# A single-token attention kernel that streams 825 MB: last scores before the last value sums, longer wo rows, and a 14 : 18 split of the scores between VectorE and TensorE

## The chip, the cores and the metric

One core of a Trainium2 chip. The metric is the device time of one launch in microseconds (us), as the median of several launches. PE is the TensorE matmul engine, PEld its weight load, DVE VectorE, ACT ScalarE, SP the engine whose queue issues the DMAs. Runs are compared with runs of the kernel before on the same chip in the same rounds.

## The reference, cut to what matters

```
x: (1, 1, 640)   k_cache, v_cache: (1, 32 heads, 32768 keys, 192)   bf16
q   = layernorm(x) @ wq                              # 32 heads x 192
p   = softmax(q . k_cache * 192**-0.5)               # one query row per head
o   = p @ v_cache                                    # (32 * 192)
h   = x + o @ wo
out = h + relu(layernorm(h) @ w1) @ w2               # 640 -> 1536 -> 640
```

Each byte of the two caches is used once. They are 805 MB of the 825 MB that are read.

## The kernel before: the parts that matter

A load brings 8192 keys of one head: 128 partitions x 64 keys ("columns") x 192 values, 24,576 B per partition. It is worked on as two chunks of 32 columns. Of a chunk, DVE scores 12 columns (multiply by the broadcast query, then reduce), and PE scores 20 (transpose K, ACT copies the transposes from PSUM, then matmuls with q). The value sums `pv` of a chunk run on PE one chunk later. The last head ends in smaller loads of 40, 16 and 8 columns.

```
full = [(JL, [(J, 20), (J, 20)])] * (Sk // (P * JL))       # (columns, of them on PE)
ends = full[:-1] + [(40, [(20, 12), (20, 12)]), (16, [(16, 10)]), (8, [(8, 4)])]
NEND = 3
...
wo_view = A_wo.rearrange("(b p) n -> p b n", p=P)          # 3 rows of 1280 B per partition
...
# o_turn: the scaled outputs of two heads become three columns
for b in range(3):
    for i in range(2):
        nc.tensor.matmul(ps[:, b:b + 1], lhsT=src[:, i, b * P:(b + 1) * P], rhs=ident_f[0:2, i:i + 1], ...)
...
# main loop over chunks g
if end == 0 and c0 == 0:                  # the last three K, then the last three V, then w1 and w2
    for i in range(NEND): load_k(ld + i)
    for i in range(NEND): load_v(ld + i)
    load_w("w1", ...); load_w("w2", ...)
...
transposes(g)
if g > 0:
    pv(g - 1)
scores_pe(g)
sc = scores_dve(g)
...
exp_dve(g, sc)
# after the loop
den_mm(H - 1); den_rec(H - 1)
pv(G - 1)
o_scale(H - 1); o_turn(H - 1); project(H // 2 - 1)
# then the dense layers
```

The softmax here doesn't subtract the row's maximum and nothing guards it: scores larger than these inputs give would overflow.

Of the kernel before, what the change touches and what calls it, by code (L numbers as in the profile page):

```python
# [13 lines left out]
def kernel(  # L14
# [12 lines left out]
    nc = tc.nc  # L27
    P = nc.NUM_PARTITIONS

    Bsz, Sq, D = A_x.shape  # L30
    _, H, Sk, Dh = A_k_cache.shape
# [9 lines left out]
    JL = 64  # L41
    J = 32
# [2 lines left out]



    full = [(JL, [(J, 20), (J, 20)])] * (Sk // (P * JL))
    ends = full[:-1] + [(40, [(20, 12), (20, 12)]), (16, [(16, 10)]), (8, [(8, 4)])]
    NEND = 3  # L50
    loads = []
    chunks = []
    for h in range(H):
        k0 = c = 0
# [8 lines left out]
            k0 += P * jl  # L63
        assert k0 == Sk
    G = len(chunks)
    NCH = [sum(1 for q in chunks if q[0] == h) for h in range(H)]
    NCM = max(NCH)
    NBM = max(q[5] for q in chunks) * Dh // P
# [4 lines left out]
    vpool = ctx.enter_context(tc.tile_pool(name="vpool", bufs=3))  # L73
# [3 lines left out]
    tsb = ctx.enter_context(tc.tile_pool(name="tsb", bufs=2))  # L77
    prp = ctx.enter_context(tc.tile_pool(name="prp", bufs=1))
    scp = ctx.enter_context(tc.tile_pool(name="scp", bufs=3))
    pcp = ctx.enter_context(tc.tile_pool(name="pcp", bufs=3))  # L80
    small = ctx.enter_context(tc.tile_pool(name="small", bufs=2))
    tps = ctx.enter_context(tc.tile_pool(name="tps", bufs=3, space=bass.MemoryType.PSUM))
    sps = ctx.enter_context(tc.tile_pool(name="sps", bufs=1, space=bass.MemoryType.PSUM))
# [4 lines left out]
    def mm_bank(shape, dtype, name):  # L88
        return mps.tile(shape, dtype, tag="mm", name=name)

    k_hd = A_k_cache.rearrange("b h s d -> (b h) s d")
    v_hd = A_v_cache.rearrange("b h s d -> (b h) s d")
    wq_view = A_wq.rearrange("(c p) n -> p c n", p=P)
    wo_view = A_wo.rearrange("(b p) n -> p b n", p=P)


    x_row = const.tile([DT, P], bf16)
# [5 lines left out]
    vt_t = {}  # L103

    def load_wq(gq):
        t = wqp.tile([P, DT * QG * Dh], bf16, tag="wq", name="wq")
        t = t[:].rearrange("p (c n) -> p c n", c=DT)
        nc.sync.dma_start(out=t, in_=wq_view[:, :, gq * QG * Dh:(gq + 1) * QG * Dh])
        wq_t[gq] = t

    def load_wo(pr):
        t = wop.tile([P, 3, D], bf16, name="wo")
        nc.sync.dma_start(out=t[:], in_=wo_view[:, 3 * pr:3 * pr + 3, :])
        wo_t[pr] = t

    def load_part(ld, src, pool, tag, name):
        h, k0, jl = loads[ld]
        if ld == len(loads) - 1:
            pool, tag, size = wqp, "wq", DT * QG * Dh
        else:  # L120
            size = JL * Dh
        t = pool.tile([P, size], bf16, tag=tag, name=name)
        nc.sync.dma_start(out=t[:, 0:jl * Dh], in_=src[h, k0:k0 + P * jl, :].rearrange("(p j) d -> p (j d)", p=P))
        return t

    def load_k(ld):
        kt_t[ld] = load_part(ld, k_hd, kpool, "kt", "kt")

    def load_v(ld):
        vt_t[ld] = load_part(ld, v_hd, vpool, "vt", "vt")  # L130

    w_t = {}

    def load_w(name, src, pool, tag, pieces):
        n, N = src.shape[0] // P, src.shape[1]
        assert n * N <= JL * Dh and n % pieces == 0
        t = pool.tile([P, JL * Dh], bf16, tag=tag, name=tag)
        v = t[:, 0:n * N].rearrange("p (c n) -> p c n", n=N)
        for i in range(pieces):
            c0, c1 = i * n // pieces, (i + 1) * n // pieces  # L140
            nc.sync.dma_start(out=v[:, c0:c1], in_=src.rearrange("(c p) n -> p c n", p=P)[:, c0:c1])
        for c in range(n):
            w_t[name, c] = v[:, c, :]
# [6 lines left out]
    ident_f = const.tile([P, P], f32)  # L150
# [40 lines left out]
    with tc.manual_schedule():  # L191
# [19 lines left out]
        def q_spread(h):  # L211
            r = rows_e[h % 2]
            qbps = mm_bank([P, Dh + 4], f32, "qbps")
            nc.tensor.matmul(qbps[:, 0:Dh], lhsT=ones_row[:], rhs=r[0:1, 0:Dh], start=True, stop=True)
            for i in range(4):
                nc.tensor.matmul(qbps[:, Dh + i:Dh + i + 1], lhsT=r[0:1, i * P:(i + 1) * P],
                                 rhs=ones_row[0:1, 0:1], start=True, stop=True)
            qb = qbp.tile([P, Dh], bf16, name="qb")
            nc.scalar.copy(out=qb[:], in_=qbps[:, 0:Dh])
            qm = qbp.tile([P, 4], bf16, name="qm")  # L220
            nc.scalar.copy(out=qm[:], in_=qbps[:, Dh:Dh + 4])
            qb_t[h], qm_t[h] = qb, qm
# [6 lines left out]
        def transposes(g):  # L229
            h, c, ld, c0, jc, jp = chunks[g]  # L230
            kt = kt_t[ld]
            NB = jp * Dh // P
            kT = tsb.tile([P, NBM, P], bf16, name="kT")
            for b0 in range(0, NB, 8):
                nb = min(8, NB - b0)
                tp = tps.tile([P, 8, P], bf16, name="tp")
                for b in range(nb):
                    off = (c0 + jc - jp) * Dh + (b0 + b) * P
                    nc.tensor.transpose(out=tp[:, b, :], in_=kt[:, off:off + P], identity=ident_b[:])  # L239
                nc.scalar.copy(out=kT[:, b0:b0 + nb, :], in_=tp[:, 0:nb, :])  # L240
            kT_t[g] = kT
# [18 lines left out]
        def scores_dve(g):  # L260
            h, c, ld, c0, jc, jp = chunks[g]
            kt = kt_t[ld]
            JD = jc - jp
            qb = qb_t[h]
            pr = prp.tile([P, JDM, Dh], f32, name="pr")
            nc.vector.tensor_tensor(out=pr[:, 0:JD, :], in0=kt[:, c0 * Dh:(c0 + JD) * Dh].rearrange("p (j d) -> p j d", d=Dh),  # L266
                                    in1=qb[:].unsqueeze(1).to_broadcast([P, JD, Dh]), op=A.mult)
            sc = scp.tile([P, J], f32, name="sc")
            nc.vector.reduce_sum(out=sc[:, 0:JD], in_=pr[:, 0:JD, :], axis=mybir.AxisListType.X)  # L269
            return sc  # L270
# [9 lines left out]
        def pv(g):  # L280

            h, c, ld, c0, jc, jp = chunks[g]
            JD = jc - jp
            vt, pA, pB = vt_t[ld], pA_t.pop(g), pB_t.pop(g)
            if c == 0:
                o_t[h] = ops.tile([2, 2 * Dh], f32, name="o_ps")
            o = o_t[h]
            order = list(range(JD, jc, 2)) + list(range(0, JD, 2))
            for i, j in enumerate(order):
                p = pA[:, j:j + 2] if j < JD else pB[:, j - JD:j - JD + 2]  # L290
                first = c == 0 and i == 0
                last = c == NCH[h] - 1 and i == len(order) - 1
                nc.tensor.matmul(o[:], lhsT=p, rhs=vt[:, (c0 + j) * Dh:(c0 + j + 2) * Dh], start=first, stop=last)  # L293
# [25 lines left out]
        def o_turn(h):  # L319
            if h % 2 == 0:  # L320
                return
            pr = h // 2
            src = o_pair[pr % 2]
            ps = mm_bank([P, 3], f32, "oT_ps")
            for b in range(3):
                for i in range(2):
                    nc.tensor.matmul(ps[:, b:b + 1], lhsT=src[:, i, b * P:(b + 1) * P], rhs=ident_f[0:2, i:i + 1],  # L327
                                     start=(i == 0), stop=(i == 1))
            oT = small.tile([P, 3], bf16, tag="oT", name="oT")
            nc.vector.tensor_copy(out=oT[:], in_=ps[:])  # L330
            oT_t[pr] = oT
# [12 lines left out]
        q_spread(0)  # L344
        for g in range(G):
            h, c, ld, c0, jc, jp = chunks[g]
            end = ld - (len(loads) - NEND)
            if end == 0 and c0 == 0:
                for i in range(NEND):
                    load_k(ld + i)  # L350
                for i in range(NEND):
                    load_v(ld + i)

                load_w("w1", B_w1, kpool, "kt", 1)
                load_w("w2", B_w2, vpool, "vt", 2)
            elif end < 0 and c0 == 0 and g > 0:
                load_k(ld)
                load_v(ld)
            if c == 1 and h % 2 == 0:
                load_wo(h // 2)  # L360
            if c == 3 and h % QG == QG - 2 and h + 2 < H:
                load_wq(h // QG + 1)
            transposes(g)
            if g > 0:
                pv(g - 1)
            scores_pe(g)
            sc = scores_dve(g)
            if c == 0 and h > 0:
                den_mm(h - 1)
                den_rec(h - 1)  # L370
                o_scale(h - 1)
            if c == 1 and h > 0:
                o_turn(h - 1)
            if c == 2 and h > 0 and h % 2 == 0:
                project(h // 2 - 1)
            if c == 4 and h + 1 < H:
                q_rows(h + 1)
            if c == 5 and h + 1 < H:
                q_spread(h + 1)
            exp_dve(g, sc)  # L380
        den_mm(H - 1)
        den_rec(H - 1)
        pv(G - 1)
        o_scale(H - 1)
        o_turn(H - 1)
        project(H // 2 - 1)
# [55 lines left out]
```

## Time and profile before

| | kernel before |
|---|---|
| time, median of 3 | 1954.45 us (1954.04 to 1954.61) |
| profiled span | 1952.3 us |
| moved by DMA | 827.85 MB, mean 424 GB/s |
| PE, DVE, ACT busy | 82%, 69%, 55% |
| last full K load landed ("L4") | 1912.08 |
| last value sum done | 1940.65 (28.57 after L4) |
| from there to the end | 11.65 us |

The busy shares are averages over a run in which every engine waits for loads. What sets the end are the three last rows: when the stream of loads delivers the last full K load, how long the work on the last five loads takes after it, and a closing chain of small dependent steps.

### The profile page before, as it was taken

What the parts mean: (1) busy time and instruction counts of PE and PEld (TensorE: products, weight loads), DVE (VectorE), ACT (ScalarE), POOL (GpSimd) and SP (SyncE); (2) the same over time, 40 slices, a digit from 0 to 9 for tenths busy, and PEclk for the clock granted to TensorE, in tenths of its full rate; (3) what the DMA queues carried; (4) which work ended last, traced back from release to release, by engine and by line L of the source; (5) the groups of instructions that cost most, each with busy time, mean ns of one, the idle gap of its engine ahead of it and who ended that gap; (6) DMA issues with size and microseconds to landing.
All of it is one profiled execution on the core that took longest, in us unless ns stands there. A gap on an engine that the chain in (4) does not pass through costs nothing.

```text
span 1952.3 us, 44906 instructions
## 1 busy us (share of the span) xinstructions
PE 1594.4 (82%) x20392; PEld 1122.4 (57%) x20392; DVE 1338.0 (69%) x654; ACT 1067.5 (55%) x2223; POOL 0.7 (0%) x6
## 2 busy tenths in 40 slices
PE   6887887878788788787888877888788887887887
PEld 4655565555556556555555655655555565565655
DVE  5766777667666676676767666777666766676675
ACT  4555555555555555555655555555555555555554
POOL 0000000000000000000000000000000000000000
PEclk9989889989998889998988989899899989898998
DMA  9999999999999999999999999999999999999996
GB/s 405 431 429 429 430 431 430 429 429 431 431 430 428 430 431 430 431 429 431 430 429 430 429 431 430 430 431 424 431 431 428 425 421 431 427 430 426 430 421 253
DMA packets 51522, 827.85 MB, mean 424 GB/s; under 512 B 4612, under 2 KB 17412, under 8 KB 18564
## 3 DMA queue, kind: packets, MB, share of 16 engines
q1 hardware_dynamic: 51332, 824.99, 99.0%
q8 instruction: 159, 2.61, 0.5%
q14 instruction: 31, 0.25, 0.0%
HBM read 824.97 MB, written 0.00 MB: 423 GB/s over the span
## 4 chain that ended last, share of the span: by engine, by line
DMA 77%; PE 17%; ACT 4%; DVE 1%; issue 1%; SPq 0%; ACTq 0%
DMA kt<-in_A_k_cache_dram 75%; PE o_ps L293 8%; PE tp L239 6%; ACT kT L240 3%; DMA vt<-in_A_v_cache_dram 1%; DVE pr L266 1%; PE sp L249 1%; PE sp L253 1%; PE sp L251 1%; PE qps L205 0%; ACT pA L276 0%; ACT pB L256 0%; DVE o_pair L314 0%; PE oT_ps L327 0%; ACT row_e L208 0%
## 5 line engine op out<-in xcount | busy, mean ns | idle before, releaser
L240 ACT COPY kT<-tp 128x1024 bf16<-128x1024 bf16 (+1 forms) x1025 | 905.2, 966 | 343.1 <-PE tp L239 340.2
L266 DVE TENSOR_TENSOR pr<-kt,qb 128x2304 f32<-128x2304 bf16 (+1 forms) x258 | 655.0, 2539 | 483.3 <-DMA kt<-in_A_k_cache_dram 479.9
L239 PE MATMUL tp<-ident_b,kt 128*128 128x128 bf16 x7677 | 599.3, 242 | 342.8 <-DMA kt<-in_A_k_cache_dram 269.7
L239 PEld LDWEIGHTS <-kt 128*128 128x128 bf16 x7677 | 531.1, 110 | 381.2 <-DMA kt<-in_A_k_cache_dram 280.2
L269 DVE TENSOR_REDUCE sc<-pr 128x12 f32<-128x2304 f32 (+1 forms) x258 | 654.3, 2536 | 27.6 <-ACT kT L240 1.4
L293 PE MATMUL o_ps<-vt,pB 128*2 128x384 bf16 x2559 | 498.8, 346 | 2.6 <-DMA vt<-in_A_v_cache_dram 2.6
L293 PEld LDWEIGHTS <-pB 128*2 128x2 bf16 x2559 | 203.8, 87 | 226.9 <-issue 65.9
L256 ACT ACTIVATE pB<-sp 128x20 bf16<-128x20 f32 (+1 forms) x258 | 48.4, 188 | 492.4 <-PE sp L253 492.4
L293 PE MATMUL o_ps<-vt,pA 128*2 128x384 bf16 x1537 | 291.9, 326 | 0.0
L249 PEld LDWEIGHTS <-kT 128*128 128x128 bf16 x2559 | 196.1, 96 | 85.7 <-issue 84.7
L249 PE MATMUL sp<-qm,kT 128*128 128x2 bf16 x2559 | 218.6, 164 | 0.5 <-ACT kT L240 0.5
L251 PE MATMUL sp<-qm,kT 128*128 128x1 bf16 x2559 | 215.0, 163 | 0.0
L253 PE MATMUL sp<-qm,kT 128*128 128x1 bf16 x2559 | 215.0, 163 | 0.0
L251 PEld LDWEIGHTS <-kT 128*128 128x128 bf16 x2559 | 198.7, 96 | 0.0
L293 PEld LDWEIGHTS <-pA 128*2 128x2 bf16 x1537 | 129.1, 84 | 120.8
L253 PEld LDWEIGHTS <-kT 128*128 128x128 bf16 x2559 | 197.4, 96 | 0.0
L276 ACT ACTIVATE pA<-sc 128x12 bf16<-128x12 f32 (+1 forms) x258 | 52.8, 205 | 0.0
L256 ACT ACTIVATION_READ_ACCUMULATOR pB<-sp 128x1 f32 x258 | 50.1, 194 | 0.0
L276 ACT ACTIVATION_READ_ACCUMULATOR pA<-sc 128x1 f32 x258 | 49.3, 191 | 0.0
L305 DVE TENSOR_REDUCE rec<-den 128x1 f32<-128x20 f32 x32 | 5.7, 179 | 60.2 <-PE den L299 60.2
L315 ACT ACTIVATE o_pair<-o_ps,rec 2x192 f32<-2x192 f32 x32 | 13.2, 412 | 26.9 <-DVE o_pair L314 26.9
L327 PE MATMUL oT_ps<-ident_f,o_pair 2*128 2x1 f32 x192 | 24.2, 247 | 0.1
(60 smaller groups left out, 191.4 us busy)
## 6 DMA issues: line engine op xcount, KB each, us to landing
kt<-in_A_k_cache_dram SPq DMA_DIRECT2D x127, 3072.0 KB, 35.7
vt<-in_A_v_cache_dram SPq DMA_DIRECT2D x127, 3072.0 KB, 31.4
wq<-in_A_wq_dram SPq DMA_DIRECT2D x8, 960.0 KB, 34.7
wo<-in_A_wo_dram SPq DMA_DIRECT2D x16, 480.0 KB, 31.2
kt<-in_A_k_cache_dram SPq DMA_DIRECT2D x1, 1920.0 KB, 30.7
vt<-in_A_v_cache_dram SPq DMA_DIRECT2D x1, 1920.0 KB, 25.4
kt<-in_B_w_dram SPq DMA_DIRECT2D x1, 1920.0 KB, 17.1
vt<-in_B_w_dram SPq DMA_DIRECT2D x2, 960.0 KB, 13.3
```

The source lines that it names most:

```text
L239: nc.tensor.transpose(out=tp[:, b, :], in_=kt[:, off:off + P], identity=ident_b[:])
L240: nc.scalar.copy(out=kT[:, b0:b0 + nb, :], in_=tp[:, 0:nb, :])
L249: nc.tensor.matmul(sp[:, 2 * i:2 * i + 2], lhsT=kT[:, 3 * i + 1, :], rhs=qm[:, 1:3], start=True, stop=False, skip_group_check=True)
L251: nc.tensor.matmul(sp[:, 2 * i:2 * i + 1], lhsT=kT[:, 3 * i, :], rhs=qm[:, 0:1], start=False, stop=False, skip_group_check=True)
L253: nc.tensor.matmul(sp[:, 2 * i + 1:2 * i + 2], lhsT=kT[:, 3 * i + 2, :], rhs=qm[:, 3:4], start=False, stop=True, skip_group_check=True)
L256: nc.scalar.activation(out=pB[:, 0:JP], in_=sp[:, 0:JP], func=F.Exp, scale=SCALE, accum_out=dsums[:, h, 2 * c + 1:2 * c + 2])
L266: nc.vector.tensor_tensor(out=pr[:, 0:JD, :], in0=kt[:, c0 * Dh:(c0 + JD) * Dh].rearrange("p (j d) -> p j d", d=Dh), in1=qb[:].unsqueeze(1 ...
L269: nc.vector.reduce_sum(out=sc[:, 0:JD], in_=pr[:, 0:JD, :], axis=mybir.AxisListType.X)
L276: nc.scalar.activation(out=pA[:, 0:JD], in_=sc[:, 0:JD], func=F.Exp, scale=SCALE, accum_out=dsums[:, h, 2 * c:2 * c + 1])
L293: nc.tensor.matmul(o[:], lhsT=p, rhs=vt[:, (c0 + j) * Dh:(c0 + j + 2) * Dh], start=first, stop=last)
L315: nc.scalar.activation(out=dst[:, 1, n0:n0 + Dh], in_=o[:, Dh:2 * Dh], func=F.Copy, scale=s[0:2, 1:2])
L327: nc.tensor.matmul(ps[:, b:b + 1], lhsT=src[:, i, b * P:(b + 1) * P], rhs=ident_f[0:2, i:i + 1], start=(i == 0), stop=(i == 1))
```

## The change

Its intent: take PE work off (14 of 32 columns on DVE), move wo in fewer, longer packets, and let no K work of the last loads wait for V. The V load of the last 40 columns (the first of the last three V loads) is also split in two.

```diff
-    full = [(JL, [(J, 20), (J, 20)])] * (Sk // (P * JL))
+    full = [(JL, [(J, 18), (J, 18)])] * (Sk // (P * JL))
...
+    ENDS = [g for g in range(G) if chunks[g][2] >= len(loads) - NEND]
...
-    wo_view = A_wo.rearrange("(b p) n -> p b n", p=P)
+    wo_view = A_wo.rearrange("(g p b) n -> g p b n", p=P, b=3)
...
     def load_v(ld):
-        vt_t[ld] = load_part(ld, v_hd, vpool, "vt", "vt")
+        parts = [(q[3], q[3] + q[4]) for q in chunks if q[2] == ld] if ld >= len(loads) - NEND else None
+        vt_t[ld] = load_part(ld, v_hd, vpool, "vt", "vt", parts)      # one DMA per chunk
...
-  lhsT=src[:, i, b * P:(b + 1) * P]
+  lhsT=src[:, i, b:3 * P:3]
...
-            if g > 0:
+            if g > 0 and g - 1 not in ENDS:
                 pv(g - 1)
...
-        pv(G - 1)
+        for g in ENDS:
+            pv(g)
```

(The pool of probabilities grows from 3 to 6 buffers, for the deferred sums.)

More of the change, by code (lines that the diff above doesn't have):

```diff
@@ L79 @@
     scp = ctx.enter_context(tc.tile_pool(name="scp", bufs=3))
-    pcp = ctx.enter_context(tc.tile_pool(name="pcp", bufs=3))
+    pcp = ctx.enter_context(tc.tile_pool(name="pcp", bufs=6))
     small = ctx.enter_context(tc.tile_pool(name="small", bufs=2))
@@ L112, in load_wo, with load_part @@
         t = wop.tile([P, 3, D], bf16, name="wo")
-        nc.sync.dma_start(out=t[:], in_=wo_view[:, 3 * pr:3 * pr + 3, :])
+        nc.sync.dma_start(out=t[:], in_=wo_view[pr])
         wo_t[pr] = t
-    def load_part(ld, src, pool, tag, name):
+    def load_part(ld, src, pool, tag, name, parts=None):
         h, k0, jl = loads[ld]
@@ L122, in load_part @@
         t = pool.tile([P, size], bf16, tag=tag, name=name)
-        nc.sync.dma_start(out=t[:, 0:jl * Dh], in_=src[h, k0:k0 + P * jl, :].rearrange("(p j) d -> p (j d)", p=P))
+        rows = src[h, k0:k0 + P * jl, :].rearrange("(p j) d -> p (j d)", p=P)
+        for j0, j1 in parts or [(0, jl)]:
+            nc.sync.dma_start(out=t[:, j0 * Dh:j1 * Dh], in_=rows[:, j0 * Dh:j1 * Dh])
         return t
@@ L326, in o_turn @@
                 for i in range(2):
-                    nc.tensor.matmul(ps[:, b:b + 1], lhsT=src[:, i, b * P:(b + 1) * P], rhs=ident_f[0:2, i:i + 1],
+                    nc.tensor.matmul(ps[:, b:b + 1], lhsT=src[:, i, b:3 * P:3], rhs=ident_f[0:2, i:i + 1],
                                      start=(i == 0), stop=(i == 1))
```

## The prediction

> **What bounds the kernel now.** First the 40 slices of the span, then the DMA queues, then the chain that ended last.
>
> ```profile
> PE   6887887878788788787888877888788887887887
> DVE  5766777667666676676767666777666766676675
> DMA  9999999999999999999999999999999999999996
> GB/s 405 431 429 429 430 431 430 429 429 431 431 430 428 430 431 430 431 429 431 430 429 430 429 431 430 430 431 424 431 431 428 425 421 431 427 430 426 430 421 253
> ...
> q1 hardware_dynamic: 51332, 824.99, 99.0%
> q8 instruction: 159, 2.61, 0.5%
> ...
> DMA 77%; PE 17%; ACT 4%; DVE 1%; issue 1%; SPq 0%; ACTq 0%
> ```
>
> The DMA row is full and some 430 GB/s move in every slice but the first and the last: 825 MB at 430 GB/s are 1918 of the 1952.3 us. PE and DVE stand at 6 to 8 tenths. So two things only can move the time: what the DMA engines have to do, and the last slice, where they run dry.
>
> The last slice I read from the timeline and from windows. Columns of the windows: stretch, length, busy (instructions) of PE, its weight loads, DVE, ACT, POOL, then granted clock, DMA share, GB/s.
>
> ```profile
> 1893.43 12.61 SPq L123 DMA_DIRECT2D kt<-in_A_k_cache_dram  x3
> 1906.10 13.78 SPq L123 DMA_DIRECT2D vt<-in_A_v_cache_dram  x3
> ...
> 1912.17 2.56 DVE L266 TENSOR_TENSOR pr<-kt,qb 128x2304 f32<-128x2304 bf16 x1 [4.36 <-DMA kt<-in_A_k_cache_dram]
> 1914.83 2.55 DVE L269 TENSOR_REDUCE sc<-pr 128x12 f32<-128x2304 f32 x1
> ...
> 1924.21 1.76 DVE L266 TENSOR_TENSOR pr<-kt,qb 128x1536 f32<-128x1536 bf16 x1 [1.57 <-DMA kt<-in_A_k_cache_dram]
> ...
> 1910.40:1913.80 3.40, 1.68 (x16) 1.68 (x17) 1.63 (x1) 0.55 (x1) 0.00 (x0) 0.50 0.98 419
> 1913.80:1917.20 3.40, 3.40 (x22) 2.15 (x21) 3.30 (x2) 3.00 (x4) 0.00 (x0) 0.50 0.58 248
> 1917.20:1924.00 6.80, 6.54 (x84) 4.32 (x83) 5.30 (x3) 4.02 (x8) 0.00 (x0) 1.00 0.75 272
> 1924.00:1931.00 7.00, 6.80 (x105) 4.72 (x103) 6.55 (x4) 3.80 (x12) 0.00 (x0) 1.00 0.95 366
> ...
> PE o_ps L293 <- DMA vt<-in_A_v_cache_dram: 0.8, 1, 0.8
> ```
>
> The reader is to see: the last full K load lands just before 1912.17 (call this moment L4). From there PE is busy almost without a break (6.54 of 6.80, 6.80 of 7.00 us), and the wait for V that the change wants to avoid is 0.8 us, once. PE's value sums end at 1940.65, and a fixed chain of 11.65 us (turn, projection, layer norm, two dense layers, output) leads to 1952.3.
>
> **A second bound, hidden in the 99%.** The trace records the sixteen completion updates of each load, one per DMA engine. For the first K load they lie at 13.0 to 13.6 us. For the K load issued at 1874.79 eight lie at 1890.3 to 1894.6 and eight at 1910.3 to 1912.1. Half the engines have fallen some 20 us behind. They are those that also fetch instructions: the late ones step back in turn, by about 1.4 us at a time. 159 fetches over 8 engines are 20 each, 28 us. A load counts as landed with its slowest engine, so these eight set the pace. In the packet records they are back to back to the end: from 1912 the remaining loads land at 1919.4, 1924.1, 1926.1, 1927.0, 1931.5, 1933.4, 1934.4, 1939.1, 1941.5 and 1944.0, as their sizes ask.
>
> **What the Trainium skill says.** "Runtime: NRT & Kernel Launch", Instruction fetch mechanics: an engine's instructions come in 16 KiB blocks of 256, over a DMA queue of its own, and the cost is mostly hidden. The count agrees (PE's 40,315 program rows / 256 = 157.5; the page shows 159 packets); hidden it is not here, at 1.4 us on a saturated engine. "DMA: Bandwidth & Descriptors", Why small descriptors are slow: a fixed cost per packet. The trace agrees and shows it small: from start to start a 1280-B packet takes 52 ns, a 3072-B one 118 ns, a 24,576-B one 908 ns. "TensorE: Matmul & The Clock Gate", Part 1: half clock after an idle window of about 3.4 us, full clock after a busy one. The trace agrees, but is stricter: at 1910.4 the clock fell to 0.50 after a window in which PE was still half busy, and came back at 1917.2. "VectorE: DVE Perf Modes", The perf-mode tier table: a reduce runs at one element per cycle. Here 2304 elements take 2.55 us and 1536 take 1.75, thus 0.2 us per column of 192.
>
> **Part by part.**
> 1. wo rows of 3840 B. 16 loads x 24 packets x 52 ns = 20.0 us per engine become 16 x 8 x about 146 ns (3 x 1280 B at the rate of large packets, 142 ns, and some 4 ns) = 18.7. All of it lies on the bound: -1.3 us.
> 2. 18 instead of 20 columns on PE. Each of some 254 full chunks loses 3 transposes and 3 score matmuls, each with its weight load: 12 rows, 3,048 in all, matching the program's 37,267 PE rows. 3,048 / 256 = 12 fetches fewer, 1.5 on each of the eight slow engines, at 1.4 us: -2.1 to -2.3 us, on the bound. PE's own saving (about 0.25 us a chunk) only lengthens its waits.
> 3. 14 instead of 12 columns on DVE. Two instructions of 2.95 instead of 2.55 us: a load costs DVE 4 x 2.95 + 0.3 = 12.1 us, where a K and V pair arrives every 14.6 us. DVE goes from 69% to about 80%, still beside the loads. K buffers come free 1.2 us later, at 9.1 after landing, against a backlog of more than 20 us on the slow engines: nothing.
> 4. Last scores first. L4 comes 3.5 us earlier, near 1908.6, from parts 1 and 2. Then, in us after L4. DVE: two full chunks to 12.2 (the next K piece lands at 12.0), two of 8 columns to 19.5, then 22.4 and 24.4. PE: first full chunk at half clock, as now, to 7.6; second to 13.1; first short chunk with the last undeferred value sums to 17.6. After that nothing fills PE while ACT copies transposes: short chunk two ends at 21.0, the next at 24.0, the last at 25.7; the exponentials at 26.2. Only then come the denominators (0.4 us) and 32 deferred value sums at 0.173 us: 5.5 us, where today 4 sums (0.75 us) follow. V is there (22.3). End at 32, against 28.6 today (1940.65 - 1912.08): +3.4 us.
> 5. Clock. Between 18.7 and 26 PE would be busy 30 to 48% of a window, less than the half that cost it the clock at 1910.4. Then the deferred sums start at half clock, and regain it after 3.5 to 5 us, as the trace shows for other restarts: about +2.2 us more, and +0.4 in the last scores.
>
> Sum: -3.5 + 3.4 + 2.6 = +2.5 us if the clock falls; about -0.1 if it does not; about -1.5 if it does not and the first chunk runs at full clock too (end at 30.7 to 31.1, set by DVE).
>
> **The rivals.** (a) The intent holds: V waits held up K work and the end shrinks by 3 to 6 us. For it: the chain of waits runs through the V load that landed at 1931.5, with 9.1 us of work behind it. Against: the wait itself is 0.8 us and PE's work is not reduced, only moved behind the last score. It would make 1949 to 1951. (b) The loads set the end: w2 lands at 1944.0 and its use starts at 1947.5, so it has 3.5 us to spare; with the loads 3.5 us earlier this stays hidden, and nothing changes. (c) DVE becomes the bound in the steady part: 12.1 of 14.6 us speaks against it; a head's first chunk adds under 1 us. If it did, 1% or more would be lost. (d) The stream gains nothing: another engine of the eight keeps its fetches, or packets cost as before; then the end's +2.5 to +6 stands alone, 1957 to 1960.
>
> **Range and chances.** Three to one for the falling clock: 0.75 x 2.5 + 0.25 x -0.8 = +1.7. I take off 0.7 for the chance of (a), since the change was made with it in mind: +1.0, thus 1955.5 us. The range 1951.5 to 1959.0 holds (a) in its milder form and most of (d). Two per cent are 39 us, more than the whole end after L4's 28.6 us, so beyond 2% either way only a bound I have not seen could do it.
>
> **What would show it.** Step 1 and 2: the page shows near 146 instruction packets; the loads before the end land 3 to 4 us earlier, at the same GB/s of 430. Step 3: DVE near 80%, groups of 2688 elements at 2.95 us, no wait of PE for it before the end. Step 4: the last scores are through some 26 us after L4, then one unbroken run of 32 value sums. Step 5: granted clock of 0.5 in that run, sums of over 0.3 us. I am wrong if the clock stays full there, if the sums wait for V, or if the loads are not earlier.

## The result, and the profile after

The changed kernel took 1955.64 us (median of 4, 1955.30 to 1956.15), the kernel before on the same chip 1954.24 (1953.99 to 1954.61): 1.4 us more. The ratio is 1.0007, with a 95% interval of 0.999 to 1.0025: the same at the 2% threshold.

The page of the changed kernel, slices, queues and chain:

```profile
DVE  6877888778878787877888777887788778788785
...
GB/s 407 429 430 430 430 430 432 429 431 431 430 430 430 430 430 432 429 427 433 430 432 431 428 430 432 431 429 430 431 428 429 427 425 429 430 429 429 432 406 229
...
q8 instruction: 147, 2.41, 0.4%
...
DMA 77%; DVE 12%; PE 9%; ACT 1%; issue 0%; SPq 0%; DVEq 0%; ACTq 0%
```

The stream runs at the same 430 GB/s. DVE rose from 69% to 79% and now stands in the chain with 12%. That share lies in the stream and not in the end; a stretch of the chain in order of time (start, us, what):

```profile
1863.95 2.97 DVE pr L270
...
1867.01 2.96 DVE sc L273
1870.00 2.97 DVE pr L270
...
1873.02 34.70 DMA kt<-in_A_k_cache_dram
1907.72 0.05 issue
1907.77 3.06 PE tp L243 x27
```

DVE frees a K buffer 9 us after its load has landed, and the next K load is issued at once. But then that load takes 34.70 us to land, because the eight slow DMA engines still have earlier loads to deliver: by their completion updates they had at least 20.3 us of such work left at every issue that can be read, from 100 us to that of the last full K load. So an earlier issue would not have brought the load earlier, and these 12% are no sign that DVE bounds the stream. There are 12 instruction packets fewer.

The end, in windows (stretch, length, busy and count of PE, PEld, DVE, ACT, POOL, then granted clock, DMA share, GB/s), and the largest wait of PE's scores there (us in total, times, longest us):

```profile
1912.60:1924.30 11.70, 11.44 (x146) 7.29 (x145) 11.37 (x6) 6.37 (x15) 0.00 (x0) 1.00 0.87 320
1924.30:1929.60 5.30, 3.37 (x74) 2.90 (x74) 5.06 (x4) 4.32 (x13) 0.00 (x0) 1.00 0.88 329
1929.60:1933.60 4.00, 2.07 (x29) 1.63 (x27) 2.35 (x3) 2.33 (x10) 0.00 (x0) 0.50 0.73 255
1933.60:1936.40 2.80, 2.80 (x10) 1.09 (x10) 0.34 (x2) 0.00 (x0) 0.00 (x0) 0.50 0.79 301
1936.40:1940.40 4.00, 3.96 (x24) 1.85 (x22) 0.00 (x0) 0.00 (x0) 0.00 (x0) 0.99 0.43 158
...
PE sp L253 <- ACT kT L244: 2.3, 3, 0.9
```

From 1924.3 PE is no longer full: 3.37 of 5.30 and 2.07 of 4.00 us, where it had been 6.80 of 7.00 in the kernel before: its scores wait for ACT's copies of the transposes, and no value sums are left to fill the gap. The clock drops to 0.50 at 1929.6. The denominators come at 1933.09, and then the 32 sums run alone, some ten of them in the first 2.80 us, at half clock. No wait for V is left. By the three terms:

| profiled run | before | after | difference |
|---|---|---|---|
| L4 | 1912.08 | 1907.72 | -4.36 |
| L4 to last value sum | 28.57 | 32.64 | +4.07 |
| closing chain | 11.65 | 13.04 | +1.39 |
| span | 1952.3 | 1953.4 | +1.1 |

The closing chain should have been fixed. It grew in its first step, the turn, which takes the wo permutation by reading every third element. The turn's weight loads, before and after (duration ns min/median/max):

```profile
L327 PEld LDWEIGHTS oT_ps<-ident_f,o_pair x192: 181/187/187, 148.3 to 1942.1; 2*128 2x128 f32 x192
```

```profile
L331 PEld LDWEIGHTS oT_ps<-ident_f,o_pair x192: 246/256/325, 147.1 to 1942.9; 2*128 2x128 f32 x192
```

The turn ended 2.85 us after the last value sum instead of 1.76. Of the other 0.3 us, 0.2 are the layer norm's matmuls, which met the half clock (0.57 us in the chain against 0.37).

### The profile page after: what moved, and what is told of

The parts are those of the page before. It is cut to its first block, busy times and chain, and to the rows that moved or that the text cites. A ratio compares the mean times of both kernels' runs of the same rounds, so it can differ in the third digit from the quotient of the medians.

```text
span 1953.4 us, 41859 instructions
## 1 busy us (share of the span) xinstructions
PE 1568.3 (80%) x18868; PEld 1084.6 (56%) x18868; DVE 1540.4 (79%) x654; ACT 994.1 (51%) x2223; POOL 0.7 (0%) x6
## 4 chain that ended last, share of the span: by engine, by line
DMA 77%; DVE 12%; PE 9%; ACT 1%; issue 0%; SPq 0%; DVEq 0%; ACTq 0%
DMA kt<-in_A_k_cache_dram 77%; DVE pr L270 8%; PE o_ps L297 4%; DVE sc L273 3%; PE tp L243 3%; ACT kT L244 1%; PE sp L253 0%; PE sp L257 0%; PE sp L255 0%; PE oT_ps L331 0%; DVE o_pair L318 0%; PE den L303 0%; PE qps L209 0%; SPq L126 0%; PE h1ps L400 0%
## 5 line engine op out<-in xcount | busy, mean ns | idle before, releaser
L244 ACT COPY kT<-tp 128x1024 bf16<-128x1024 bf16 (+1 forms) x1025 | 823.1, 886 | 345.5 <-PE tp L243 343.5
L270 DVE TENSOR_TENSOR pr<-kt,qb 128x2688 f32<-128x2688 bf16 (+1 forms) x258 | 756.5, 2932 | 304.6 <-DMA kt<-in_A_k_cache_dram 300.7
L243 PE MATMUL tp<-ident_b,kt 128*128 128x128 bf16 x6915 | 563.7, 247 | 369.0 <-DMA kt<-in_A_k_cache_dram 293.9
L273 DVE TENSOR_REDUCE sc<-pr 128x14 f32<-128x2688 f32 (+1 forms) x258 | 755.8, 2929 | 27.6 <-DVE pr L270 1.0
L243 PEld LDWEIGHTS <-kt 128*128 128x128 bf16 x6915 | 495.0, 113 | 406.0 <-DMA kt<-in_A_k_cache_dram 304.5
L297 PE MATMUL o_ps<-vt,pA 128*2 128x384 bf16 x1791 | 333.9, 326 | 0.0
L260 ACT ACTIVATE pB<-sp 128x18 bf16<-128x18 f32 (+1 forms) x258 | 48.0, 186 | 519.3 <-PE sp L257 519.3
L253 PEld LDWEIGHTS <-kT 128*128 128x128 bf16 x2305 | 177.2, 96 | 87.7 <-issue 84.1
L257 PE MATMUL sp<-qm,kT 128*128 128x1 bf16 x2305 | 196.2, 163 | 1.0 <-ACT kT L244 1.0
L255 PE MATMUL sp<-qm,kT 128*128 128x1 bf16 x2305 | 196.2, 163 | 0.0
L255 PEld LDWEIGHTS <-kT 128*128 128x128 bf16 x2305 | 179.7, 96 | 0.0
L257 PEld LDWEIGHTS <-kT 128*128 128x128 bf16 x2305 | 178.5, 96 | 1.2 <-ACT kT L244 1.2
L280 ACT ACTIVATE pA<-sc 128x14 bf16<-128x14 f32 (+1 forms) x258 | 54.2, 210 | 37.4 <-DVE sc L273 37.2
```

The costliest lines, as they stand in the source:

```text
L243: nc.tensor.transpose(out=tp[:, b, :], in_=kt[:, off:off + P], identity=ident_b[:])
L244: nc.scalar.copy(out=kT[:, b0:b0 + nb, :], in_=tp[:, 0:nb, :])
L253: nc.tensor.matmul(sp[:, 2 * i:2 * i + 2], lhsT=kT[:, 3 * i + 1, :], rhs=qm[:, 1:3], start=True, stop=False, skip_group_check=True)
L255: nc.tensor.matmul(sp[:, 2 * i:2 * i + 1], lhsT=kT[:, 3 * i, :], rhs=qm[:, 0:1], start=False, stop=False, skip_group_check=True)
L257: nc.tensor.matmul(sp[:, 2 * i + 1:2 * i + 2], lhsT=kT[:, 3 * i + 2, :], rhs=qm[:, 3:4], start=False, stop=True, skip_group_check=True)
L260: nc.scalar.activation(out=pB[:, 0:JP], in_=sp[:, 0:JP], func=F.Exp, scale=SCALE, accum_out=dsums[:, h, 2 * c + 1:2 * c + 2])
```

## The experiments

Twelve kernels ran, in three groups, and all gave correct results; the idle matmuls of three of them write PSUM that nothing reads. Times are medians; "vs" is the kernel before in the same rounds. The three last columns come from the one profiled run of each kernel. Of the kernel before there is one profile only, but its medians on the three chips of these groups lie within 0.2 us (1954.42 to 1954.57).

| run | time | vs | L4 | L4 to last sum | closing chain |
|---|---|---|---|---|---|
| (before) | 1954.24 | | 1912.08 | 28.57 | 11.65 |
| (changed) | 1955.64 | 1954.24 | 1907.72 | 32.64 | 13.04 |
| order_only | 1958.87 | 1954.57 | 1911.83 | 33.42 | 11.75 |
| dve14_only | 1954.32 | 1954.57 | 1908.78 | 31.23 | 12.49 |
| wo_only | 1954.27 | 1954.57 | 1910.39 | 29.06 | 13.05 |
| no_order | 1954.10 | 1954.57 | 1907.65 | 31.68 | 12.97 |
| pe_rows | 1979.39 | 1954.43 | 1924.29 | 37.65 | 11.86 |
| pe_time | 1960.44 | 1954.43 | 1914.05 | 32.80 | 11.65 |
| turn_packed | 1955.20 | 1954.43 | 1907.82 | 32.59 | 12.69 |
| warm | 1954.69 | 1954.43 | 1907.51 | 31.15 | 12.84 |
| split_v | 1950.56 | 1954.42 | 1907.73 | 27.81 | 13.36 |
| fill | 1950.84 | 1954.42 | 1907.53 | 29.31 | 12.46 |
| best | 1949.88 | 1954.42 | 1907.78 | 27.46 | 13.16 |
| best16 | 1949.04 | 1954.42 | 1906.10 | 27.48 | 13.72 |

The closing chain grows for two reasons, which the table mixes: the strided turn, and the moment at which the clock falls to half in the chain. In dve14_only, which keeps the old turn, the clock fell 0.9 us after the last sum and the turn ended after 2.38 us; in the kernel before it fell after 3.8 us and the turn ended after 1.77. In best16 it fell after 0.9 us as well. Not all of that column can therefore be put down to the edits.

### Each part alone: order_only, dve14_only, wo_only, no_order

My theory at this point: the stream gives 3.5 to 4.4 us, and the deferral takes them back. The rival: something else takes them.

order_only is the kernel before with the deferral and the split V load (the edit in short, not word for word):

```diff
-                pv(g - 1)                       # every chunk, one later
+                pv(g - 1) if g - 1 not in ENDS  # the last four after the loop
+  the V load of 40 columns as two DMAs of 20
```

> The kernel before with the deferred value sums and the split V loads alone; 12 DVE columns and the old wo rows stay. My theory: the loads are not a bit earlier (last full K load landed, L4, near 1912), the value sums end 32 to 33 us after L4 instead of 28.6, about +3.5 to +4.5 us, thus near 1958.2; 32 sums in one run, partly at half clock. Rival (the order is harmless or helps, another part gave the gain back): 1952 to 1954.5.

It took 1958.87, 4.3 us more than before: as expected, and the rival falls. L4 is unmoved, the end is 4.85 us longer. Its windows show the same two things as the changed kernel's, PE half idle and then the clock:

```profile
1916.80:1929.00 12.20, 11.94 (x174) 8.04 (x172) 10.20 (x6) 6.92 (x18) 0.00 (x0) 1.00 0.84 328
1929.00:1937.00 8.00, 4.13 (x76) 3.32 (x73) 6.88 (x6) 6.37 (x21) 0.00 (x0) 0.93 0.88 312
1937.00:1944.60 7.60, 7.60 (x32) 3.32 (x32) 0.34 (x2) 0.00 (x0) 0.00 (x0) 0.63 0.49 180
```

dve14_only changes one number:

```diff
-    full = [(JL, [(J, 20), (J, 20)])] ...
+    full = [(JL, [(J, 18), (J, 18)])] ...
```

> The kernel before with 14 of 32 columns on DVE alone. My theory: 12 instruction fetches fewer, the slowest DMA engine gets one or two fewer at 1.4 us, L4 1.4 to 2.8 us earlier and the end with it: near 1951.7. Rival (DVE at 80 per cent delays K buffers or the last scores): 1954.2 or more.

This missed. L4 did come 3.3 us earlier, but the time fell by 0.25 us only; in the profile the end took back 2.7 us and the closing chain 0.8 (the early fall of the clock, above). The rival as I had put it (DVE late) is not what happened either: DVE was through its last reduce at 1933.21, 5.7 us ahead of the denominators. A wait that was small before had grown:

```profile
PE o_ps L293 <- DMA vt<-in_A_v_cache_dram: 2.7, 1, 2.7
```

Before, this line said 0.8 us. PE, with earlier K and fewer transposes, now comes to the first value sums of the last 40 columns sooner than their V does, which landed at 1929.53, only 2.0 us earlier than in the kernel before (1931.52).

wo_only has the longer rows and the strided turn:

```diff
-    wo_view = A_wo.rearrange("(b p) n -> p b n", p=P)
+    wo_view = A_wo.rearrange("(g p b) n -> g p b n", p=P, b=3)
-  lhsT=src[:, i, b * P:(b + 1) * P]
+  lhsT=src[:, i, b:3 * P:3]
```

> The kernel before with the 3840-B wo rows and their strided weight loads in the turn alone. My theory: -1.3 us of packets, +1.1 us in the last turn, because its weight loads read every third element and wait for both halves: near 1954.0. Rival (packets alone count): 1952.9.

Near the expectation: L4 came 1.7 us earlier, the end took 0.5 us longer (here too the V wait had grown, from 0.8 to 2.0 us), and the closing chain 1.4 us longer. What is left, 0.3 us less in the medians and 0.2 us more in the profiled runs, is within the noise.

no_order is the changed kernel with `pv` in its old place and V unsplit:

> The changed kernel with the value sums in their old place (wo rows and 14 DVE columns stay). My theory: L4 as in the changed kernel, near 1907.7; end about 28.6 us later plus the turn's 1.1: near 1951.2. Rival (the gain upstream is lost whatever the order): 1954 to 1955.6.

Missed, as dve14_only: 1954.10, 0.5 us under the kernel before, not 3. L4 is the changed kernel's, but the end takes 31.68 us. The waits and windows of its end:

```profile
PE o_ps L293 <- DMA vt<-in_A_v_cache_dram: 3.1, 1, 3.1
```

```profile
1925.50:1928.70 3.20, 0.07 (x2) 0.08 (x2) 3.06 (x3) 1.77 (x3) 0.00 (x0) 1.00 0.90 339
1928.70:1932.10 3.40, 3.40 (x15) 1.22 (x15) 3.16 (x4) 0.00 (x0) 0.00 (x0) 0.50 0.62 221
1932.10:1939.40 7.30, 6.69 (x84) 3.97 (x82) 0.58 (x4) 3.94 (x15) 0.00 (x0) 1.00 0.71 259
```

PE stands for 3.1 us, and for that the clock halves, so that the ten sums after the wait take 3.4 us instead of 1.8. So the four runs leave a puzzle: without the deferral the gain of the stream is lost to a wait for V; with it, the wait is gone and the gain is lost to the long run at the end. The deferral with its split and the earlier stream do not add: the pair costs 4.3 us on the kernel before, but 1.9 us (1.4 + 0.5, each against its own kernel before) on the other two parts.

### The stream: pe_rows and pe_time

Is it the number of PE instructions, through their fetches, that moves L4, or PE's time? pe_rows adds 30 one-column matmuls per chunk to the kernel before, pe_time 5 of 384 columns, meant to take about the same PE time:

```diff
+            for i in range(30):      # pe_time: range(5), 384 columns
+                nc.tensor.matmul(sp[:, 64:65], lhsT=ident_b[:], rhs=kt_t[ld][:, 0:1], start=True, stop=True, ...)
```

> The kernel before plus 30 matmuls of one column (each with its weight load) per chunk into unused PSUM: about 15,500 PE program rows, 0.8 us of PE time per chunk, which PE has idle. My theory: some 60 instruction packets more, 7.6 on each of eight DMA engines at 1.4 us: about +10 us, near 1964.5, with the last full K load landing that much later and PE still idle between loads. Rival (instruction fetch is hidden; only PE time counts and it has slack): 1954.2, within 1 us.

> The kernel before plus 5 matmuls of 384 columns per chunk: the same 0.8 us of PE time per chunk, but only about 2,600 rows, 10 instruction packets more. My theory: one step of 1.4 us, at most two: 1955.5 to 1957. Rival (PE time is what costs in the run with 30 small ones): the same loss as there.

The instruction lines of the two pages (packets, MB, share):

```profile
q8 instruction: 219, 3.59, 0.6%
```

```profile
q8 instruction: 169, 2.77, 0.5%
```

For L4 the theory holds. 60 packets more put it 12.2 us later, 10 packets more 2.0 us: 7.5 and 1.25 on each of eight engines, thus some 1.6 us apiece, a little over the 1.4 that I had read from the landings. PE's busy time grew by 176 us in pe_rows and by 134 us in pe_time, 1.3 to 1, where L4 moved 6 to 1. Could L4 have moved because a busier PE freed the buffers, and so issued the loads, later? The completion updates say no: at every issue that can be read, from 100 us to that of the last full K load, the slow eight engines still had at least 15.6 us (pe_rows) and 16.1 us (pe_time) of earlier loads to deliver. So PE's time is not the cause there. For the whole time I was wrong in both: +25 and +6 us instead of +10 and +1.3 to +2.8. After L4 the work on the last chunks is PE's, and there the added matmuls are not all hidden: in pe_time the end grew by 4.2 us, some 0.97 us of matmuls and 0.37 us of wait ahead of them per chunk. In pe_rows PE was moreover 5.2 us late for the last full K load (landed 1924.29, transposes from 1929.49), after a chunk at half clock, and its launches scatter from 1972.6 to 1986.0. I don't claim to know that scatter's cause.

### The closing chain and the clock: turn_packed and warm

turn_packed permutes in the scaling instead, so that the turn's weight loads are contiguous again; all else is the changed kernel:

```diff
+  perm = lambda t: t.rearrange("q (b p) -> q p b", b=3)[:, p0:p0 + Dh // 3, :]     # strided write
-  lhsT=src[:, i, b:3 * P:3]
+  lhsT=src[:, i, b * P:(b + 1) * P]
```

> The changed kernel with the permutation moved from the turn's weight loads to the scaling before it, so that the weight loads are contiguous again. My theory: the turn's loads drop from 256 to 187 ns, but the first one still waits for both halves: 0.8 to 1.1 us off, 1954.5 to 1954.8. Rival (the stride costs nothing): 1955.6.

It took 0.8 us more than the kernel before, where the changed kernel took 1.4 more: 0.6 us less, a little short of the expectation. The weight loads are back at 187 ns, but the two strided scalings now take 0.53 and 0.58 us instead of 0.41 each, and the first third of the turn still waits for both heads. In the kernel before it needed the first head alone, and began before the last scaling.

warm is the changed kernel with five idle matmuls ahead of the scores of each of the last three chunks, for the clock:

```diff
+            if g in ENDS[1:]:
+                for i in range(5):
+                    nc.tensor.matmul(sp[:, 64:448], lhsT=ident_b[:], rhs=kt_t[ld][:, 0:384], start=True, stop=True, ...)
```

> The changed kernel with 5 idle matmuls of 384 columns between transposes and scores of each of the last three chunks, where PE waits for ACT. My theory: the clock stays at 1.0 in the last scores and the 32 sums, which take 5.6 instead of 6.7 us; 0.3 us lost by the extra work: 1.0 to 1.5 us off, near 1954.4. Rival (the run of sums is bound by something else than the clock): 1955.6 or more.

```profile
1924.90:1933.30 8.40, 6.88 (x101) 4.97 (x97) 6.64 (x6) 6.60 (x22) 0.00 (x0) 1.00 0.84 304
1933.30:1938.70 5.40, 5.36 (x33) 2.60 (x32) 0.34 (x3) 0.00 (x0) 0.00 (x0) 1.00 0.64 241
```

The clock stays at 1.00 and the 32 sums take 5.36 us instead of 6.72. Adding useless work to PE took about 1.1 us off (0.3 over the kernel before, against 1.4). The launches lie at 1953.3, 1953.7 and three times near 1954.7; the profile is of the quicker kind. That the clock costs the 32 sums of the changed kernel 1.4 us is shown by the two traces; the 1.1 us of the medians alone would not show it, since the intervals overlap (ratios 0.999 to 1.0025 and 0.9987 to 1.0012).

### Taking the V wait away without the deferral: split_v, fill, best, best16

The deferral came with a split of the V load of the last 40 columns. split_v keeps that, the 14 columns and the wo rows, and puts `pv` back:

```diff
-            if g > 0 and g - 1 not in ENDS:
+            if g > 0:
                 pv(g - 1)
-        for g in ENDS:
-            pv(g)
+        pv(G - 1)
```

> The kernel with 14 DVE columns and the 3840-B wo rows, value sums in their old place, but with the split V loads (which came with the deferral). My theory: without the deferral PE stood 2.7 to 3.1 us before the first value sums of the last 40 columns, waiting for all of that V load; its first half lands 2.3 us earlier, the wait falls under 1 us, the clock stays up: 2 to 3.5 us off the run without the deferral, near 1951.3. Rival (the V wait only hides another wait, DVE or ACT, that ends at the same time): 1954.

1950.56 us, 3.9 us under the kernel before. Wait and windows:

```profile
PE o_ps L296 <- DMA vt<-in_A_v_cache_dram: 0.5, 1, 0.5
```

```profile
1925.00:1932.00 7.00, 6.51 (x92) 4.38 (x89) 6.62 (x6) 5.07 (x15) 0.00 (x0) 1.00 0.80 279
1932.00:1936.50 4.50, 3.46 (x26) 1.79 (x23) 0.84 (x4) 1.97 (x11) 0.00 (x0) 1.00 0.82 306
```

The first half of the 40 columns landed at 1926.41, and PE waited 0.5 us for it. PE stays full, the clock stays up, and after the denominators four sums remain. The end takes 27.81 us against 31.68 without the split. So the puzzle is solved: the wait was for the second half of a load whose first half was enough.

split_v is also the changed kernel without its deferral (and the larger pool that came with it), so the two show what the deferral alone does on this stream. It brings the denominators forward by 1.3 us (25.37 us after L4 instead of 26.67), which is what it was meant for, and puts 28 more sums behind them; the value sums end 4.8 us later after L4, and the medians differ by 5.3 us (+1.4 against -3.9).

fill keeps a deferral, but of two chunks instead of to the end (with the packed turn):

```diff
             if g > 0 and g - 1 not in ENDS:
                 pv(g - 1)
+            elif g - 2 in ENDS:
+                pv(g - 2)
-        for g in ENDS:
+        for g in ENDS[-2:]:
             pv(g)
```

> The changed kernel with packed turn and the deferred sums put two chunks behind the scores instead of all at the end (20 of the 32 run before the denominators). My theory: 12 sums instead of 32 after the last score, at full clock, the last scores 1 to 2 us later: 2.5 to 3.5 us off the changed kernel, near 1952. Rival (the sums only move the last scores back by what they take): 1954.5 to 1955.

1950.84 us: it is not the deferral as such that costs, but leaving PE without work before the denominators and with 32 sums after them. (About 0.35 us of the gain over the changed kernel is the packed turn's, by the closing chains of turn_packed and the changed kernel.)

best is split_v with the packed turn, best16 the same with 16 of 32 columns on DVE:

> As the run with split V loads, with the packed turn as well. My theory: 0.4 us less than it, near 1950.9, below both kernels. Rival: no different from the kernel before, 1954.

> As the run before this one, with 16 instead of 14 of 32 columns on DVE. My theory: another 12 instruction packets fewer, 1.4 to 2.8 us earlier at the last full K load; DVE at 13.7 of 14.5 us per load still beside the loads, though the last scores now wait for DVE (13.7 us after L4 instead of 12.2): near 1949.5. Rival (DVE becomes the bound, at 94 per cent of a load pair with the work of a head's first chunk on top): 1956 or more.

1949.88 and 1949.04 us, both below both kernels, and best16 5.4 us (0.28%, interval 0.16% to 0.41%) under the kernel before. In best16 the page counts 135 instruction packets, L4 comes 1.7 us earlier again, and DVE, 90% busy, is still beside the loads: at every issue the slow eight DMA engines had at least 20.1 us of earlier loads left (19.9 in the kernel before). A share of 90% did not make it the bound, since each load leaves it some time; it would not bear 18 columns, I estimate: at 0.2 us per column and instruction, 18 columns make 4 x 3.75 + 0.3 = 15.3 us per load, over the 14.6 that a K and V pair takes.

## Why the prediction was right or wrong

The time was right: 1955.5 predicted, 1955.64 measured, range 1951.5 to 1959.0. By its steps:

- **The bound, and the eight slow engines: right.** In the changed kernel's last full K load eight completion updates lie at 1887.5 to 1893.0 and eight at 1907.4 to 1907.7. pe_rows and pe_time moved L4 by the number of instruction packets and not by PE's time. That the slow eight are those that fetch is inferred from these steps; no record names the engine of a fetch. Nor does the prediction reconcile 28 us of fetches with a lag of 20: the other eight engines had at times only 1.2 us of loads left at an issue, so the buffers may have capped the lag (not tested). (The program rows that the prediction counts, 40,315 and 37,267, stand in no run. The traces have 40,784 and 37,736 matmuls and weight loads; their difference is the same 3,048, and 40,784 / 256 = 159.3 fits the 159 packets better than 157.5.)
- **Step 1, wo rows, -1.3 us: right in the stream** (L4 1.7 us earlier in wo_only), **but the step left out the turn.** "A fixed chain of 11.65 us" failed: 13.04, with 1.1 us more in the turn alone. With it the wo part is worth nothing beyond the noise.
- **Step 2, 12 fetches fewer, -2.1 to -2.3 us: right in kind** (147 packets, 12 fewer), **under-sized:** 3.3 us at L4 in dve14_only. The wrong term is "1.5 on each": an engine loses whole fetches, and the slowest engine sets the pace; two at the 1.6 us of pe_rows are 3.2. The updates fit this: the slow eight lay between 1910.32 and 1912.08 in the kernel before, and between 1908.43 and 1908.78 in dve14_only. It was not tested further.
- **"All of it lies on the bound": wrong as a statement of what the parts are worth.** I said that the stream's gain reaches the end. In no_order it did not: a wait for V of 0.8 us became 3.1, and the clock fell behind it. I had weighed that wait by its size in the kernel before, although step 4 itself made PE arrive earlier.
- **Step 3, DVE beside the loads: right.** 79%, no loss in the stream; best16 shows room beyond.
- **Step 4, the run of 32 sums after the denominators: right in kind, over-sized by about one us.** I put the denominators at 26.6 us after L4, with the scores slowed by the clock; they came at 25.37. V was there.
- **Step 5, the clock: right in kind, over-sized by about one us.** It fell before the sums, as said, but came back 2.8 us into them, not 3.5 to 5: 6.72 us instead of 7.7. warm shows it by taking it away.
- **The sum.** Stream -4.36 (said -3.5), end +4.07 (said +6.0), chain +1.39 (said 0): +1.1 us in the profiles, +1.4 in the medians, where the scenario of the falling clock said +2.5 and the weighted number +1.0. The errors are of one to two microseconds each and cancel in part, so the 0.1 us between number and median is luck; that the signs of the first two terms and the range are right is not.
- **Rival (a), that the V wait mattered, was half right.** On the kernel before, the deferral with the split lost 4.3 us (order_only); the split alone was not run there, where the wait was 0.8 us. On the stream of the changed kernel 3.4 us were to be gained (split_v against no_order, each against its kernel before), but by the split, not by the deferral that came with it. I had not looked at the split at all.

## What to carry to other kernels

When loads bound a kernel, an instruction of a busy engine is also a load: fewer instructions on the engine with the most of them can be worth more than the time that they take. At the end of such a kernel, split the last loads so that work can begin on their first part, rather than push the work that waits behind everything else; an engine that runs dry there loses its clock as well. And weigh a small wait by what the same change does to the arrival of its waiter: 0.8 us became 3.1 when PE reached the wait sooner.

## What the Trainium skill lacked or had wrong

- "Runtime: NRT & Kernel Launch", Instruction fetch mechanics, calls the cost of a fetch mostly hidden. Under a saturated stream it is not: 60 packets more moved the last full K load by 12.2 us, 12 fewer by 3.3 us. No page says that PE's fetches seem to fall on eight of the sixteen DMA engines only (inferred, as said above), and that these come to lie 20 us behind the others (completion updates at 1890.3 to 1894.6 and 1910.3 to 1912.1 of one load).
- "TensorE: Matmul & The Clock Gate", Part 1, gives an idle window of about 3.4 us as what lowers the clock. Here half a window was enough: PE busy 1.84 of the 3.4 us before the fall at 1929.6, and 1.74 of the 3.4 us before the fall at 1910.4 in the kernel before. No sharp limit comes out of the traces: ahead of the 78 falls in the kernel before, PE was busy for 0 to 79% of 3.4 us (median 47%), and 5 of the 385 windows on the same grid that kept the clock were under half busy too (busy as the profile models it). The return agrees with Part 1: the clock came back 3.3 us (at 1936.4) and 4.8 us (at 1912.6) after PE's work had set in again in the changed kernel.
- "SBUF — State Buffer", Door 1, says that each access that crosses to a new 16-byte line pays a penalty, puts how far one can stride for free at 4 fp32 elements, and gives no number for a weight load. Here fp32 weight loads with a step of three elements were not free: 256 ns instead of 187. On the writing side, scalings of 2 x 192 fp32 values that were written with a step of 128 elements took 0.53 instead of 0.41 us on DVE and 0.58 instead of 0.41 on ACT.
- "DMA: Bandwidth & Descriptors", Why small descriptors are slow, works the cost of a packet out for 256 B only. With 1280-B rows there was little left: three such packets take 3 x 55 ns, one of 3840 B takes 149, and 16 loads in longer rows moved the last full K load by 1.7 us of 1912.
